# Seven products instead of eight for the up projection, on operands shared with q and k, and the down and out products moved behind it

## The chip, the cores and the metric

The kernel runs on one core of a Trainium2 chip. A core has a matrix engine (TensorE, PE in the profile), three engines for elementwise work (VectorE or DVE, ScalarE or ACT, GpSimd or POOL), a queue that issues most transfers (SyncE, SP), and 16 DMA engines between DRAM and the on-chip memory. Matrix products land in PSUM, which holds eight tiles of 128x512 numbers of 32 bits here. The metric is the device time of one execution in microseconds. All arithmetic is on 32-bit numbers.

## The reference

The input x has 2048 positions of 512 numbers. The kernel computes `x + s * silu(g)`, where s is a sliding attention over the normalised x and g a dense layer with squared ReLU over the same normalised x:

```python
xn = layernorm(x)                                   # 2048 x 512
q, k, v = split(xn @ wqkv)                          # 32 heads of 16
# every position looks back at 8 positions, 2 apart
logits = sum_d q[s] * k[s - 2*w] / 4                # w = 0..7; -1e9 before the start
o = sum_w softmax(logits)[w] * v[s - 2*w]
s = o @ wo                                          # 512 x 512
h = xn @ w1 + b1                                    # w1 is 512 x 1792, "up"
g = relu(h)**2 @ w2 + b2                            # w2 is 1792 x 512, "down"
out = x + s * silu(g)
```

## The kernel before, in words

**Numbers in two parts.** Each matrix operand is split into a high part of fewer bits (written by ACT) and the low part that is left (a subtraction on DVE or POOL). A product is then three matmuls, `PASSES`: high x high, high x low, low x high. A product over 512 input numbers is four slices of 128 of them times three passes, 12 matmuls of 128x512.

**Phase 1** goes over 16 tiles of 128 positions, in pairs. Each tile is normalised, transposed into `pxT` in PSUM, split into `xt` or `xT`, and multiplied with the weights of q, k and v. For the pairs in `SEVEN` (tiles 4 to 15) `pair_of_seven` (L800) computes the q and k of both tiles as a 2x2 block product with seven block products in place of eight, on sums of quarters of the two tiles (`copy_quarter`, `sums`, `high_sums`, `low_sums`) and sums of weights (`T1` to `T4`). For the pairs in `VSEVEN` (6 to 13) v is made in the same way, on halves of its columns. Results go through `stg` to DRAM (`sq`, `sk`, `sv`). The split operands of tiles 4 to 15 also go to DRAM (`sx`).

**Phase 2** goes over four chunks c of 512 positions, and over the 14 tiles f of 128 up features. `up(c, f)` (L604) is 12 matmuls of w1's tile with the chunk's operands `xT[c]`, loaded back from `sx`; then three passes on ACT make relu and the square, and POOL (in the first chunk DVE, for f = 2 to 11: `lowh`) the low part of h. `down` (L906) multiplies h of one f with w2, four position tiles by three passes. The four sums of a chunk stay in PSUM over all f. Up and down alternate on PE. `out_product` (L942) multiplies the attention's result with wo, tile by tile, between them; `finish` multiplies with the gate and adds x.

**Attention** needs no products: it is made by DVE alone, in `attention()` (L264), in eight units of 256 positions. A unit is four multiplies and four reductions for the logits (`qk`), the softmax (`soft_a`, `soft_b`, partly on POOL and ACT), and four multiplies and four reductions for the result (`av`). `load_u` fetches the unit's q, k and v from DRAM, and `store` writes the result to `so`, from where `load_o` (L917) fetches it for the out product; `trans_o` transposes it on DVE and `lowo` makes its low part there.

**The order of the work** is fixed when the program is built. Each engine runs its instructions in the order in which they were issued. A planner keeps two clocks, one for PE and one for DVE, with a price for each instruction. `pump(margin)` (L389) puts attention instructions into DVE's order as long as the DVE clock stays under PE's clock plus the margin: `LATE` (3.0 us) in phase 1, `ROOM0` (0.5 us) in the first chunk of phase 2, `ROOM` (3.5 us) in the others. `not_before(t)` moves the DVE clock forward where an instruction must wait for PE. `load_o(u, force)` with force places attention, whatever the clocks say, until unit u is stored:

```python
while done_units[0] <= u:
    flush(None)
    pump(clock["V"] - clock["PE"] + 4000)
```

`plan` holds what is done beside each step of a pair in phase 1 (`beside`). `queue` issues a transfer on SP in program order; a transfer that has to wait holds up those behind it.

Of the kernel before, what the change touches and what calls it, by code (L numbers as in the profile page):

```python
# [41 lines left out]
HOME = {0: 10, 1: K0, 2: T1, 3: T2, 4: T3, 5: Q0, 6: Q1, 7: K1, 8: T4, 9: V0, 10: V1}  # L42

SEVEN = range(4, 16, 2)
VSEVEN = range(6, 14, 2)
# [14 lines left out]
def body(ctx: ExitStack, tc: tile.TileContext, x, wqkv, wo, w1, b1, w2, b2, out):  # L60
# [48 lines left out]
    xTa = ctx.enter_context(tc.tile_pool(name="xTa", bufs=1))  # L109
    keep = ctx.enter_context(tc.tile_pool(name="keep", bufs=1))  # L110
    wts = ctx.enter_context(tc.tile_pool(name="wts", bufs=1))
    hpool = ctx.enter_context(tc.tile_pool(name="ph", bufs=1))
# [11 lines left out]
    def piece(name):  # L124
        return keep.tile([P, 512], F32, name=name, tag="z", bufs=4)
# [11 lines left out]
    p1ctx = ExitStack()  # L137
    px, pstg, pxT = (p1ctx.enter_context(tc.tile_pool(name=n, bufs=1)) for n in ("px", "pstg", "pxT"))
    xins = {}

# [15 lines left out]
    def load_x(t):  # L156
        xins[t] = px.tile([P, D], F32, name=f"x{t}", tag="x", bufs=4)
        queue(xins[t], tile_rows(x, t))
# [5 lines left out]
    wq = [buffer(f"wq{i}", i) for i in range(10)]  # L164
# [46 lines left out]
    b2t = const.tile([P, D], F32, name="b2t")  # L211
# [5 lines left out]
    sx = {c: dram.tile([P, KT, TPC, 2, P], F32, name=f"sx{c}") for c in range(1, NCH)}  # L217
# [185 lines left out]
    w12 = {}  # L403

    def load_w(f):
        r1, r2 = (piece(f"{n}{f}") for n in ("w1r", "w2r"))
        queue(r1.rearrange("p (k c) -> p k c", c=P), w1[:, f * P:(f + 1) * P].rearrange("(k p) c -> p k c", p=P))
        queue(r2, w2[f * P:(f + 1) * P, :])
        raws[f] = r1, r2

    def next_w():

        f = len(w12)
        if f < NF:
            w12[f] = buffer(f"w{f}", HOME[f]) if f in HOME else p2.tile([P, 2, 2, 512], FR, name=f"w{f}")
            for i, r in enumerate(raws.pop(f)):
                split(w12[f][:, 0, i], w12[f][:, 1, i], r, G)
            if f + 2 < NF:
                load_w(f + 2)
# [3 lines left out]
    mv, means, rs, shifts, xn, xb, pTs, xt, xT, seen, Sf, Sp, xts = ({} for _ in range(13))  # L423
# [11 lines left out]
    def spread(t):  # L435

        means[t], rs[t], shifts[t] = (small(n, t) for n in ("mean", "rs", "shift"))
        waste = hpool.tile([P, 512], F32, name=f"waste{t}", tag="hf")
# [11 lines left out]
    def norm(t):  # L450

        src = xins.pop(t)
        if t < TURN:
            xn[t] = dst = px.tile([P, 2, D], F32, name=f"xn{t}", tag="xb", bufs=2)[:, 0]
        else:
            if t % 2 == 0:
                xn[t] = px.tile([P, 4, 2, P], F32, name=f"xn{t}", tag="xn", bufs=2)
# [11 lines left out]
    def place(t):  # L469
        if t < TPC:  # L470
            parts = xT[0][:, :, t]
        else:
            parts = xts[t] = pxT.tile([P, KT, 2, P], FR, name=f"xt{t}", tag="xt", bufs=4)
        xt[t] = parts.rearrange("p k a n -> p a k n")

    def shuffle(t):

        src = xn.pop(t)
        xb[t] = px.tile([P, 4, 2, P], F32, name=f"xb{t}", tag="xb", bufs=2)
        for a in range(4):  # L480
            queue(xb[t][32 * a:32 * a + 32].rearrange("p b e c -> p b (e c)"), src[:, a].rearrange("p e c -> p (e c)"))
        if t > TURN:
            for i in range(t + 4, min(t + 6, NT)):
                load_x(i)

# [15 lines left out]
    def highx(t):  # L501
        A.activation(xt[t][:, 0], pTs[t].rearrange("p (k n) -> p k n", k=KT), AF.Copy)

    def lowx(t):
        not_before(seen[t])
        V.tensor_sub(xt[t][:, 1], pTs[t].rearrange("p (k n) -> p k n", k=KT), xt[t][:, 0].bitcast(F32))
# [8 lines left out]
    def copy_quarter(a):  # L515

        _, pb = quarters(a)
        Sf[a] = hpool.tile([P, 4, 2 * P], F32, name=f"Sf{a}", tag="h", bufs=4)
        A.activation(Sf[a][:, 3], pb[:, 0], AF.Copy)
        seen[a, "copy"] = clock["V"] + 1600  # L520

    def sums(a, half):

        f, (pa, pb) = Sf[a], quarters(a)
# [4 lines left out]
        else:  # L529
            V.tensor_sub(f[:, 2], pa[:, 0], f[:, 3])  # L530
            V.tensor_sub(f[:, 3], pa[:, 1], f[:, 1])
        seen[a, half] = clock["V"] + 900

    def sum_parts(a, half):
        n = 2 * half
        flat = Sf[a][:, n:n + 2].rearrange("p j m -> p (j m)")
        if (a, half) not in Sp:
            Sp[a, half] = hpool.tile([P, 2, 2, 2, P], FR, name=f"S{a}_{half}", tag="h", bufs=4)
        return (*(Sp[a, half][:, i].rearrange("p j k n -> p (j k n)") for i in range(2)), flat)
# [8 lines left out]
    def part_x(t, h):  # L548
        return lambda p, i: xt[t][:, p, 2 * h + i]

    def part_s(a, j):
        return lambda p, i: Sp[a, j // 2][:, p, j % 2, i]
# [13 lines left out]
    def new_stg(t, s):  # L566
        stgs[s] = pstg.tile([P, GR, 2, CH], F32, name=f"stg{t}_{s}", tag="stg", bufs=4)

    def qkv(t, s, between=None, late=False, new=True):
# [5 lines left out]
        for n, (kt, a, b) in enumerate(order):  # L575
            PE.matmul(ps, xt[t][:, a, kt], wq[2 * s + kt // 2][:, b, kt % 2, :], start=n == 0, stop=n == 11,
# [20 lines left out]
    def load_xT(c):  # L597
        xT[c] = xTa.tile([P, KT, TPC, 2, P], FR, name=f"xU{c}", tag="xT")
        for kt in range(KT):
            queue(xT[c][:, kt].bitcast(F32), sx[c][:, kt])  # L600

    hs = {}

    def up(c, f):  # L604
        ph = psH(f"ph{c}_{f}")
        n = 0
        for kt in range(KT):
            for a, b in PASSES:
                PE.matmul(ph.rearrange("p (j n) -> p j n", n=P), w12[f][:, a, 0, kt * P:(kt + 1) * P],
                          xT[c][:, kt, :, b, :], start=n == 0, stop=n == 11)  # L610
                n += 1
        if f == NF - 1 and c + 1 < NCH:
            load_xT(c + 1)
        h = hpool.tile([P, 2, 512], FR, name=f"h{c}_{f}", tag="h", bufs=4)
        A.activation(ph, ph, AF.Relu, bias=b1t[:, f:f + 1])
        A.activation(h[:, 0], ph, AF.Square)

        pool = c or f < 2 or f > 11
        full = hpool.tile([P, 512], F32, name=f"hf{c}_{f}", tag="hf") if pool else ph
        A.activation(full, ph, AF.Square)  # L620
        if pool:
            G.tensor_sub(h[:, 1], full, h[:, 0].bitcast(F32))
        hs[f] = h, None if pool else ph, clock["PE"] + 2000

    def lowh(f):
        h, ph, t = hs[f]
        if ph is not None:
            not_before(t)
            V.tensor_sub(h[:, 1], ph, h[:, 0].bitcast(F32))

# [12 lines left out]
    xT[0] = xTa.tile([P, KT, TPC, 2, P], FR, name="xT0", tag="xT")  # L643
# [8 lines left out]
    x0 = hpool.tile([P, D], F32, name="xT0f", tag="h", bufs=4)  # L652
# [6 lines left out]
    high(xt[0][:, 0], None, x0.rearrange("p (k n) -> p k n", k=KT))  # L659
    ps = psA("pq0_1")  # L660
    for kt in range(KT):
        if kt == KT - 1:
            trans(1)
        PE.matmul(ps, x0[:, kt * P:(kt + 1) * P], raws[1, kt], start=kt == 0, stop=kt == KT - 1)
    lowx(1)
    low(xt[0][:, 0], xt[0][:, 1], x0.rearrange("p (k n) -> p k n", k=KT), V)
# [12 lines left out]
    trans(2)  # L679
    lows(2, 0)  # L680
# [3 lines left out]
    trans(3)  # L684
    lows(2, 2)
# [23 lines left out]

    vl, vr = slice(0, 256), slice(256, 512)  # L710
    v_sums, v_parts = {}, {}

    def sum_v(n):
        dst, a, b = (((0, vl), (0, vr), (0, vl)), ((2, vr), (2, vr), (0, vl)), ((0, vr), (2, vr), (0, vr)),
# [385 lines left out]
```

## Time and profile before

| what | value |
|---|---|
| median of two runs | 484.75 us (484.53 and 484.98) |
| span of the profiled execution | 482.6 us; its own time is not listed apart from the two runs' |
| PE busy | 477.1 us, 2193 matmuls |
| DVE busy | 428.1 us, 356 instructions |
| ACT busy | 240.0 us |
| POOL busy | 221.8 us |
| moved by DMA | 81.47 MB |

The span goes from the first to the last instruction of the profiled execution. The profile page gives the busy time of each engine, a strip of 40 equal slices per engine (each digit the busy share in tenths), the costliest groups of instructions, and the chain of waits that ended last. In a group, `pb<-w,h` means that tile pb was written from w and h; then come the shape, the count, the busy time, the mean time of one and the idle time just ahead. All instructions that pass through the kernel's recording helper have the line number L91, so groups are told apart by the names of their tiles. A timeline row is start, duration, engine, line, operation, tiles, shape and count, and in brackets the engine's idle time before it with what ended it.

### The profile page before, as it was taken

How to read it: one execution, taken by the hardware profiler on the slowest of the kernel's cores; microseconds unless marked ns; L12 is line 12 of the kernel's file. 1: busy time of each engine (PE TensorE's matmuls, PEld its weight loads, DVE VectorE, ACT ScalarE, POOL GpSimd, SP SyncE). 2: the span in 40 equal slices, each digit the busy share in tenths (PEclk: the TensorE clock that was granted, in tenths of full speed). 3: DMA queues.
4: the chain of work that ended last, by engine and by line, in shares of the span. 5: the costliest groups of instructions: out<-in, count | busy, mean ns of one | idle time of the engine just before them, and what ended most of it. 6: DMA issues, size and time to landing. Idle time of an engine off the chain costs nothing.

```text
span 482.6 us, 6131 instructions
## 1 busy us (share of the span) xinstructions
PE 477.1 (99%) x2193; PEld 397.0 (82%) x2193; DVE 428.1 (89%) x356; ACT 240.0 (50%) x441; POOL 221.8 (46%) x174
## 2 busy tenths in 40 slices
PE   8999999999999999999999999999999999999996
PEld 6888888888888888888888888888888888888885
DVE  5968999899599999899999999999999999999133
ACT  5548798855566545463413345342235343423240
POOL 1459852116995654337445532653334257243210
PEclk9999999999999999999999999999999999999999
DMA  8999999998769765834624843560764446040331
GB/s 277 248 233 286 271 242 290 300 298 259 209 196 251 191 180 153 254 95 127 160 63 132 187 160 107 113 178 5 184 150 117 159 109 170 0 129 4 88 104 70
DMA packets 70890, 81.47 MB, mean 169 GB/s; under 512 B 6092, under 2 KB 55500, under 8 KB 70860
## 3 DMA queue, kind: packets, MB, share of 16 engines
q1 hardware_dynamic: 69564, 73.61, 55.3%
q10 hardware_dynamic: 1296, 7.47, 6.6%
q8 instruction: 17, 0.28, 0.2%
q14 instruction: 13, 0.11, 0.1%
HBM read 50.60 MB, written 27.32 MB: 161 GB/s over the span
## 4 chain that ended last, share of the span: by engine, by line
PE 98%; DMA 1%; DVE 0%; POOL 0%; issue 0%; POOLq 0%
PE pb L91 32%; PE ph L91 32%; PE pm L91 12%; PE pq L91 9%; PE pw L91 9%; PE pv L91 4%; DMA x<-in_A_x 1%; PE pxT L91 0%; DVE z L91 0%; DVE st L91 0%; POOL rs L91 0%; DVE xn L91 0%; DVE mv L91 0%; DVE rs L91 0%; PE warm L91 0%
## 5 line engine op out<-in xcount | busy, mean ns | idle before, releaser
L91 PE MATMUL pb<-w,h 128*128 128x512 f32 x672 | 160.1, 389 | 0.0
L91 PEld LDWEIGHTS pb<-w,h 128*128 128x128 f32 x672 | 126.1, 188 | 26.2
L91 POOL TENSOR_TENSOR h<-hf,h 128x512 fp32r<-128x512 f32 x46 | 72.2, 1570 | 133.7 <-ACT hf L91 133.6
L91 PE MATMUL ph<-xU,w 128*128 128x512 f32 x504 | 120.2, 389 | 0.0
L91 ACT ACTIVATE ph<-ph,b1t 128x512 f32<-128x512 f32 x56 | 37.1, 662 | 161.3 <-PE ph L91 161.3
L91 PEld LDWEIGHTS ph<-xU,w 128*128 128x128 f32 x504 | 94.6, 188 | 19.7
L91 DVE TENSOR_TENSOR pr<-k,q 128x2048 f32<-128x2048 f32 x32 | 79.4, 2480 | 0.9 <-DMA q<-sq 0.2
L91 DVE TENSOR_TENSOR pv<-v,L 128x2048 f32<-128x2048 f32 x32 | 78.4, 2450 | 1.3 <-POOL L L91 0.7
L91 DVE TENSOR_REDUCE v<-pv 128x256 f32<-128x2048 f32 x32 | 73.1, 2283 | 0.9
L91 DVE TENSOR_REDUCE L<-pr 128x128 f32<-128x2048 f32 x32 | 72.8, 2275 | 0.5
L91 PE MATMUL pw<-wot,oT 128*128 128x512 f32 (+1 forms) x204 | 45.9, 376 | 0.0
L91 PEld LDWEIGHTS pw<-wot,oT 128*128 128x128 f32 x204 | 36.8, 188 | 7.1
L91 PE MATMUL ph<-xT,w 128*128 128x512 f32 x168 | 40.0, 389 | 0.0
L91 POOL TENSOR_TENSOR w<-w1r,w 128x512 fp32r<-128x512 f32 x14 | 24.1, 1718 | 30.9 <-ACT w L91 29.3
L91 PEld LDWEIGHTS ph<-xT,w 128*128 128x128 f32 x168 | 31.5, 188 | 6.5
L91 PE MATMUL pm<-wq,S 128*128 128x512 f32 x144 | 36.5, 391 | 0.0
L91 ACT ACTIVATE h<-ph 128x512 fp32r<-128x512 f32 x56 | 33.7, 602 | 1.8
L91 PE MATMUL pq<-wq,xT 128*128 128x512 f32 x132 | 30.8, 392 | 0.0
L91 PEld LDWEIGHTS pm<-wq,S 128*128 128x128 f32 x144 | 26.3, 188 | 4.9
L91 PEld LDWEIGHTS pq<-wq,xT 128*128 128x128 f32 x132 | 24.5, 188 | 5.8 <-ACT xT L91 0.7
L91 ACT ACTIVATE hf<-ph 128x512 f32<-128x512 f32 x46 | 27.3, 594 | 1.3 <-POOL h L91 1.3
L91 PE MATMUL pm<-wq,xt 128*128 128x512 f32 x108 | 27.6, 392 | 0.0
(96 smaller groups left out, 534.5 us busy)
## 6 DMA issues: line engine op xcount, KB each, us to landing
sx<-xt SPq DMA_DIRECT2D x12, 512.0 KB, 7.0
xU<-sx SPq DMA_DIRECT2D x12, 512.0 KB, 6.3
k<-sk SPq DMA_DIRECT2D x5, 960.0 KB, 7.1
v<-sv SPq DMA_DIRECT2D x5, 960.0 KB, 7.1
x<-in_A_x SPq DMA_DIRECT2D x16, 256.0 KB, 8.0
sk<-stg SPq DMA_DIRECT2D x8, 512.0 KB, 4.2
sq<-stg SPq DMA_DIRECT2D x8, 512.0 KB, 7.7
sv<-stg SPq DMA_DIRECT2D x8, 512.0 KB, 5.0
```

What stands on the lines that cost most here:

```text
L91: return tc.keep_in_program_order(f(*a, **k))
```

## The change

The up projection is made by seven block products. A block pairs two tiles of w1 (pair g of 7) with the even and odd tiles of a group s of 1024 positions; the seven position operands are exactly those that q and k use in phase 1. They now live in four arrays `XA`, `XB`, `SA`, `SB`, with four slots each, one for each pair of tiles. Group 0 (tiles 0 to 7) is written to DRAM by `store_x` in phase 1; group 1 stays on the chip. The first four tiles get their sums too (`keep_full`, `early_sums`, `early_parts`). v is made by plain products in all pairs.

After phase 1 comes an up stage. Group 1 comes first, then `reload` brings group 0's operands back during the last call of group 1. Each call of `ups` takes two or three pairs g through the seven products; the pre-activations u go to DRAM in `su` (`give`). The sums of w1's tiles are made on the way (`plain_w1`, `sum_w1` on DVE from the third pair on, `sums_w1`). After that come the four chunks with only down and out products; u is loaded back (`load_ut`), squared by ACT, and its low part made by POOL (`make_h`), some tiles ahead. wo is split on POOL. The core of the diff:

```diff
-VSEVEN = range(6, 14, 2)
+JOINT = (((0, 1), (2, 3), (4, 5, 6)), ((0, 1, 2), (3, 4), (5, 6)))
...
-        return keep.tile([P, 512], F32, name=name, tag="z", bufs=4)
+        return keep.tile([P, 512], F32, name=name, tag="z", bufs=12)
...
+    XA = tpool.tile([P, 4, 2, 2, 256], FR, name="XA")
+    XB = tpool.tile([P, 4, 1, 2, 256], FR, name="XB")
+    SA = tpool.tile([P, 4, 2, 2, 256], FR, name="SA")
+    SB = tpool.tile([P, 4, 2, 2, 256], FR, name="SB")
+    operands = ((XA, 0), (XA, 1), (XB, 0), (SA, 0), (SA, 1), (SB, 1), (SB, 0))
...
+    sx = [dram.tile([P, 4, n, 2, 256], F32, name=f"sx{i}") for i, n in enumerate((2, 1, 2, 2))]
+    su = [dram.tile([NF, P, 2, 512], F32, name=f"su{s}") for s in range(2)]
...
+    def plain_w1(g):
+        r0, r1 = w1raws[g]
+        pool, tag, n = home(g, 1)
+        b = pool.tile([P, 2, 3, 256], FR, name=f"w1b{g}", tag=tag, bufs=n)
+        for cols, r in ((slice(0, 2), r0), (slice(2, 3), r1[:, 256:])):
+            r = r.rearrange("p (j m) -> p j m", m=256)
+            split(b[:, 0, cols], b[:, 1, cols], r, G)
+        w1s[g] = [b]
+
+    def sum_w1(g, eng):
+        r0, r1 = w1raws[g]
+        lo, hi = slice(0, 256), slice(256, 512)
+        eng.tensor_sub(r0[:, lo], r1[:, lo], r0[:, lo])
+        eng.tensor_sub(r1[:, lo], r1[:, hi], r1[:, lo])
+        eng.tensor_sub(r1[:, hi], r1[:, hi], r0[:, lo])
+        eng.tensor_sub(r0[:, hi], r0[:, hi], r1[:, hi])
...
+    def parts(t, src):
+
+        if t % 2 == 0:
+            return [(XA[:, slot(t), :, 0], XA[:, slot(t), :, 1], src.rearrange("p (h m) -> p h m", h=2))]
+        return [(odd[t][:, 0], odd[t][:, 1], src[:, :256]), (XB[:, slot(t), 0, 0], XB[:, slot(t), 0, 1], src[:, 256:])]
...
+    def keep_full(t, src):
+        f = fulls[:, t // 2]
+        for h, q in enumerate((3, 0) if t % 2 else (1, 2)):
+            A.activation(f[:, q], src[:, h * 256:(h + 1) * 256], AF.Copy)
...
+    for a, step, f, args in ((10, 2, load_w1, (0,)), (12, 0, load_w1, (1,)), (12, 4, plain_w1, (0,)),
+                             (12, 5, sum_w1, (0, G)), (14, 1, sums_w1, (0,)), (14, 2, load_w1, (2,)),
+                             (14, 2, plain_w1, (1,)), (14, 3, sum_w1, (1, G)), (14, 4, sums_w1, (1,))):
+        at(a, step, f, *args)
...
+    def multiply(ps, g, w, j, start):
+        t, n = operands[j]
+        w, k = (w1s[g][0], w) if w < 3 else (w1s[g][1], w - 3)
+        k0 = 0
+        for i in range(2):
+            cols = slice(i * P, (i + 1) * P)
+            for a, b in PASSES:
+                PE.matmul(ps.rearrange("p (j n) -> p j n", n=P), w[:, a, k, cols], t[:, :, n, b, cols],
+                          start=start and k0 == 0, stop=k0 == 5, skip_group_check=True)
+                k0 += 1
...
+        def take(g, i, e, ps):
+            us[g, i, e] = u = piece(f"u{s}_{2 * g + i}_{e}")
+            A.activation(u, ps, AF.Identity, bias=bias(g, i))
+
+        def give(g, i, e):
+            queue(su[s][2 * g + i][:, e], us.pop((g, i, e)))
...
+        def seventh(g):
+            multiply(X[g], g, 5, 5, False)
+            take(g, 1, 1, X[g])
+            G.tensor_add(us[g, 1, 1], us[g, 1, 1], five.pop(g))
+            give(g, 1, 1)
+
+        def third(g):
+            multiply(Z[g], g, 2, 6, False)
+            not_before(clock["PE"] + 300)
+            V.tensor_add(us[g, 1, 0], us[g, 1, 0], Z[g])
+            give(g, 1, 0)
...
+        order = ((first, second, sixth, fifth, seventh, third, fourth) if len(gs) > 2
+                 else (first, fifth, sixth, second, seventh, third, fourth))
+        for product_of in order:
+            for g in gs:
+                product_of(g)
+                for f in beside.pop(0) if beside else ():
+                    f()
+                pump(ROOM0)
+            if then:
+                then(product_of.__name__)
...
+    def prepare(step, g):
+        return ((step, plain_w1, g), (step + 1, sum_w1, g, V), (step + 4, sums_w1, g))
+
+    ups(1, JOINT[0][0], tasks(14, (0, load_w1, 3), *prepare(0, 2), (5, load_w1, 4), *prepare(7, 3)))
+    ups(1, JOINT[0][1], tasks(14, *prepare(0, 4), (1, load_w1, 5), *prepare(4, 5), (5, load_w1, 6), *prepare(9, 6)))
+    ups(1, JOINT[0][2], then=reload)
...
+    def make_h(c, f):
...
+        A.activation(u, u, AF.Relu)
+        A.activation(h[:, 0], u, AF.Square)
+        A.activation(u, u, AF.Square)
+        G.tensor_sub(h[:, 1], u, h[:, 0].bitcast(F32))
+        hs[c, f] = h
...
+        room = ROOM
+        for f in range(NF):
...
+            if f >= 7:
+                load_o(c * 2, f >= 9)
...
+            if f == 11:
                 for i in range(2):
                     trans_o(t0 + i, psT(f"pT{t0 + i}"))
+            if f == 12:
                 for i in range(2):
                     lowo(t0 + i)
+                load_o(c * 2 + 1, last)
+            ahead_h(c, f)
+            if f == 0 and c == 0:
+                pass
...
+            elif f < (NF - 3 if last else NF - 2):
+                for j in range(TPC):
+                    down(c, f, j)
             pump(room)
...
+            for i in range(2):
+                out_product(t0 + i, psH(f"pw{t0 + i}"))
+                pump(room)
             for i in range(2, TPC):
+                trans_o(t0 + i, psT(f"pT{t0 + i}"))
```

More of the change, by code (lines that the diff above doesn't have):

```diff
@@ L400, in pump @@
             not_before(limit)
[L403 to L419, printed above, removed]
+    w1s, w1raws = {}, {}
@@ L595, in store_qkv @@
         done[1][t // 2] = clock["PE"]
[L597 to L629, printed above, removed]
     def highs(s, kt):
@@ L663, in body @@
             trans(1)
+            keep_full(1, pTs[1])
         PE.matmul(ps, x0[:, kt * P:(kt + 1) * P], raws[1, kt], start=kt == 0, stop=kt == KT - 1)
     lowx(1)
-    low(xt[0][:, 0], xt[0][:, 1], x0.rearrange("p (k n) -> p k n", k=KT), V)
+    for part in parts(0, x0):
+        low(*part, V)
     evacuate(0, 1, ps)
```

427 lines of the change are left out of this document (223 added, 204 removed).

## The prediction

> **What bounds the kernel now.** I read the page first, then busy time by stage, the chain of waits in order of time, and the groups and timelines of single engines around the places that the change touches.
>
> ```profile
> span 482.6 us, 6131 instructions
> ...
> PE 477.1 (99%) x2193; PEld 397.0 (82%) x2193; DVE 428.1 (89%) x356; ACT 240.0 (50%) x441; POOL 221.8 (46%) x174
> ...
> PE   8999999999999999999999999999999999999996
> ...
> DVE  5968999899599999899999999999999999999133
> ```
>
> TensorE (PE) is never idle after the start, so fewer matmuls look like a gain one for one. But the second strip shows VectorE (DVE) nearly as full from slice 12 to slice 37. Busy time by stage, with the columns in the first line:
>
> ```profile
> core 0: us, PE busy (x) PEld busy (x) DVE busy (x) ACT busy (x) POOL busy (x), PEclk, DMA share, GB/s
> 45.00:130.00 85.00, 85.00 (x453) 73.35 (x453) 77.92 (x89) 63.27 (x139) 45.00 (x45) 1.00 0.98 274
> 130.45:265.00 134.55, 134.55 (x596) 111.40 (x595) 128.79 (x81) 66.73 (x117) 74.37 (x45) 1.00 0.60 163
> 265.00:446.30 181.30, 181.30 (x802) 150.12 (x801) 178.47 (x106) 73.27 (x123) 75.47 (x46) 1.00 0.45 119
> ```
>
> From 45 to 446.3 us DVE has 401.3 us and is busy 385.2; the largest single hole is one wait of 5.7 us, shown below. So DVE finishes the attention as soon as it can, and only what follows is slack. How much, the last unit of attention and the end show:
>
> ```profile
> 423.94 0.56 SPq L343 DMA_DIRECT2D so<-v  x1
> 443.93 2.29 DVE L91 TENSOR_REDUCE v<-pv 128x256 f32<-128x2048 f32 x1
> 446.24 0.55 SPq L343 DMA_DIRECT2D so<-v  x1
> 450.08 3.64 SPq L927 DMA_DIRECT2D oq<-so  x8
> 455.98 0.73 DVE L91 STREAM_TRANSPOSE pT<-oq 128x512 f32<-128x512 f32 x1 [8.57 <-ACT hf L91]
> 473.01 5.75 PE L91 MATMUL pw<-wot,oT 128*128 128x512 f32 x36
> ...
> oq<-so SPq DMA_DIRECT2D x64, 64.0 KB, 2.0
> ...
> L91 DVE TENSOR_TENSOR oT<-pT,oT 128x512 fp32r<-128x512 f32 x13 | 8.4, 680 | 1.5 <-ACT oT L91 1.5
> ```
>
> Attention ends at T = 446.2. Its result goes to DRAM and comes back: the loads are issued until 453.7 and land 2.0 later, at 455.7, T + 9.5. Two transposes (1.46) and the first low part (0.68) make T + 11.6; the last 36 products take 5.75; from their end (478.76) to the end of the span are 3.84. If only this chain were left, the end would be T + 21.2 = 467.4. PE has 15.2 us of work more than that now, and this is all that can be won before DVE bounds the kernel.
>
> **PE's side.**
>
> ```profile
> 86.10 2.75 PE pm L91 x12
> 100.78 2.75 PE pm L91 x12
> 282.77 5.44 PE pb L91 x24
> ```
>
> A matmul of 512 columns costs 5.44/24 = 0.2267 us. Up has 4 chunks x 14 tiles x 12 = 672 matmuls; seven products of six matmuls for 7 pairs of tiles and 2 groups are 588: 84 x 0.2267 = -19.0. A pair of position tiles with q, k and v by seven repeats after 14.68 us; q and k are 42 x 0.2267 = 9.52 of it, v 5.16. Plain v is 24 x 0.2267 = 5.44, four times +0.28 = +1.1. PE alone would end the span at 482.6 - 17.9 = 464.7.
>
> **DVE's side, which I think decides.** Groups between 45 and 446.3 us (busy, mean ns, idle before):
>
> ```profile
> L91 DVE TENSOR_TENSOR pr<-k,q 128x2048 f32<-128x2048 f32 x32 | 79.4, 2480 | 0.9 <-DMA q<-sq 0.2
> L91 DVE TENSOR_TENSOR pv<-v,L 128x2048 f32<-128x2048 f32 x32 | 78.4, 2450 | 1.3 <-POOL L L91 0.7
> L91 DVE TENSOR_REDUCE L<-pr 128x128 f32<-128x2048 f32 x32 | 72.8, 2275 | 0.5
> L91 DVE TENSOR_TENSOR xt<-pxT,xt 128x512 fp32r<-128x512 f32 x10 | 6.8, 683 | 0.0
> L91 DVE TENSOR_TENSOR h<-ph,h 128x512 fp32r<-128x512 f32 x10 | 6.8, 681 | 0.0
> L91 DVE TENSOR_TENSOR Sf<-Sf,pxT 128x256 f32<-128x256 f32 x10 | 4.1, 414 | 0.2
> L91 DVE TENSOR_TENSOR wot<-rwo,wot 128x512 fp32r<-128x512 f32 x4 | 4.2, 1079 | 0.0
> L91 DVE TENSOR_TENSOR stg<-stg,pm 128x512 f32<-128x512 f32 x6 | 4.1, 685 | 7.0 <-PE pm L91 6.9
> L91 DVE TENSOR_TENSOR stg<-stg,pv 128x256 f32<-128x256 f32 x4 | 1.7, 417 | 0.4 <-PE pv L91 0.4
> ```
>
> Work: gone are ten low parts of h (6.8), four of wo (4.3), four adds for v (1.7): -12.8. New are 14 adds in `third` (x 0.685 = 9.6), `sum_w1` on DVE for five pairs, 20 subtractions of 256 columns (x 0.414 = 8.3), and six odd tiles whose low part is now two halves (2 x 0.414 - 0.683 = 0.15 each, 0.9): +18.8. Net +6.0.
>
> Waits: DVE runs in the order that the planner wrote. In the up stage, attention is placed only until PE's planned time + ROOM0 (0.5 us) and in lumps of 2.3 (the reductions) to 2.5. The add in `third` reads PE's newest product, one product (6 x 0.2267 = 1.36) after the last placing. So DVE arrives 1.36 - 0.5 = 0.86 to 0.86 + 2.3 us early, 2.0 in the middle; attention queued behind the add waits with it. The add takes 0.6, the next pair's product ends 1.36 later, and no lump fits between: 0.76 for each further pair. Six calls x 2.0 + 8 further pairs x 0.76 = +18.1. The bounds are 0, if DVE always comes late, and 6 x 3.16 + 8 x 0.76 = 25. This stage has no row before, but the same kind of add has one:
>
> ```profile
> 119.43 2.29 DVE L91 TENSOR_TENSOR pr<-k,q 128x2048 f32<-128x2048 f32 x1
> 124.07 3.46 DVE L91 TENSOR_TENSOR pr<-k,q 128x2048 f32<-128x2048 f32 x1
> 133.26 0.69 DVE L91 TENSOR_TENSOR stg<-stg,pm 128x512 f32<-128x512 f32 x1 [5.73 <-PE pm L91]
> ...
> 125.34 3.35 POOL L91 TENSOR_TENSOR w<-w2r,w 128x512 fp32r<-128x512 f32 x1
> 129.91 1.30 POOL L91 TENSOR_TENSOR w<-w2r,w 128x512 fp32r<-128x512 f32 x1
> ```
>
> There DVE stood 5.73 us for PE, because up products lay inside the last pair; the change takes those out, so -5.7. I take the middle, 18.1, because at this wait DVE was on plan and not late.
>
> Contention: the same rows show a multiply of 3.46 beside a POOL subtraction of 3.35, against 2.29 and 1.30 apart. Over 64 multiplies the means exceed 2.285 by (0.195 + 0.165) x 32 = 11.5 us, at 195 us of POOL work (45.0 + 74.4 + 75.5): 0.059 per us. New for POOL are 21 more 256-column pieces of w1, eight for two `sum_w1`, 14 adds in `seventh`, ten h and four wo; gone are the v sums:
>
> ```profile
> L91 POOL TENSOR_TENSOR h<-hf,h 128x512 fp32r<-128x512 f32 x46 | 72.2, 1570 | 133.7 <-ACT hf L91 133.6
> L91 POOL TENSOR_TENSOR stg<-stg 128x256 f32<-128x256 f32 x4 | 3.4, 854 | 0.0
> L91 POOL TENSOR_TENSOR vsum<-wqraw,vsum 128x512 fp32r<-128x512 f32 x4 | 7.1, 1805 | 0.0
> ```
>
> 29 x 0.854 + 28 x 1.57 - 10.5 = +58 us, so +3.4. Bounds: 0, and 58 x 0.9 (1.17 lost per 1.30) x 0.39 (the multiplies' share of 401 us) = 20.
>
> The Trainium skill, "SBUF — State Buffer", section "Who interferes with whom", calls this an exclusive lock between the two engines in which the loser blocks fully. The pair of long rows agrees; by that rule the sum would lie toward the upper bound only if POOL mostly came first, and the mean of all multiplies says that it mostly does not.
>
> So far +6.0 + 18.1 - 5.7 + 3.4 = +21.8: unit 6 is stored at 423.9 + 21.8 = 445.7. In the last chunk the code forces `load_o(6)` at f = 9. PE's own work from there is 84 matmuls (19.0), the last 5.75 and 3.84, so this is at 464.7 - 28.6 = 436.1; with ROOM, attention placed up to 439.6 is not forced. Unit 6 is later, so the loop places attention to its store and little more, and the transposes at f = 11 follow at once: DVE stands for the round trip of 9.5 us, less one lump of up to 4 us that the loop places beyond. I take 6.0 (bounds 0 and 9.5). T = 446.2 + 21.8 + 6.0 = 474.0, the end 495.2. The two timed runs have a median of 484.75, 2.15 above this span: **497 us**.
>
> At nothing I cost: 8 copies `keep_full` (0.4 us each, under a DVE that starts attention at 45), and six ACT passes per pair and group, 84 x 0.6 = 50 us, covered by an ACT that is half idle; if that cover fails, PE stands and DVE behind it. `store_x`, `give`, `reload` and `load_ut` put about 32 MB more through SP's queue; attention's q, k, v loads stand behind each `give` that waits for ACT, POOL or DVE. That is a rival below.
>
> In the forecast PE stands over 10 us before its last products. The Trainium skill, "TensorE: Matmul & The Clock Gate", section "What's actually happening", says that after about 3.4 us idle the clock falls to half for about as long; an estimate from that page is +1.7 us, the sum 499 instead. Every window above has a granted clock of 1.00, and no run here shows it.
>
> **Rivals.** *Late adds absorb each other* (0.23): if POOL makes DVE late, half of the 18.1 is no loss of its own. T = 446.2 + 6.0 + 9.0 - 5.7 + 3.4 = 458.9, unit 6 at 436.6 isn't forced, end 480.1: 482. For it speaks the pair of long rows, against it that the lost time comes back as contention.
>
> *PE bounds after all* (0.20, the other side): the adds in `third` cost no wait, because DVE is always behind its plan there. Then T = 446.2 + 6.0 - 5.7 = 446.5, end 467.7: 470, and no less than PE's 464.7 + 2.15 = 467. It decides when DVE's net lateness is under 5.5 us. For it: PE is at 99% and the arithmetic saved is sure. Against: DVE is at 96% from 45 on, and program order fixes its waits.
>
> *The up stage starves* (0.12).
>
> ```profile
> sx<-xt SPq DMA_DIRECT2D x12, 512.0 KB, 7.0
> GB/s 277 248 233 286 271 242 290 300 298 259 209 196 251 191 180 153 254 95 127 160 63 132 187 160 107 113 178 5 184 150 117 159 109 170 0 129 4 88 104 70
> ```
>
> In the third call 7.3 MB of operands come back, 3.1 MB of pre-activations leave and some 2.2 MB of attention move in 21 x 1.36 = 28.6 us: 440 GB/s, where no slice shows over 300. At 300 it takes 42 us, up to 14 us late: 497 + 14 = 511. Against: each operand is asked for six steps, 24.5 us, before its next use.
>
> **Numbers.** The forecast has 0.45; it spans 490 to 505, and its size is worth 2% only above 494.4. A measurement here tells 2%: below 475.1 or above 494.4. Faster: 0.20. Within 2%: 0.23 + 0.08 = 0.31. Slower: 0.37 + 0.12 = 0.49. Both signs hold much, so the range goes from PE's bound, 467, to 514, which leaves out a part of the starved case and little else.
>
> **What would show it.** Up must have 588 matmuls and PE busy fall to about 459, with idle PE near the end. DVE's adds into u must show waits for PE, some 18 us in all; attention's last reduction must lie near 474; the transposes for tiles 12 and 13 must stand for the load of unit 6. I am wrong if the last reduction stays near 447, or if PE stands inside the up stage for ACT, POOL or a load.

## The result, and the profile after

The changed kernel takes 572.92 us (571.14 and 574.70) against 484.75: 1.182 times the time, with a 95% interval of 1.173 to 1.191. The forecast was 497 with a range of 467 to 514. Timed later in three rounds it took a median of 576.88 (574.25 to 580.64), 1.191 times (1.186 to 1.196). Its executions lie 6.4 us apart where those of the kernel before lie 0.6 apart, so of a version timed once a few us are no difference.

The page of the changed kernel:

```profile
span 572.9 us, 6280 instructions
...
PE 490.7 (86%) x2037; PEld 392.3 (68%) x2037; DVE 445.6 (78%) x380; ACT 300.6 (52%) x537; POOL 290.3 (51%) x224
...
PE   8996997999898879999984978999998999932905
...
DVE  5956855889477787969869759779996998994934
...
PEclk9997998999998979999997988999998999975957
```

No engine is full any more. PE has 156 matmuls fewer, as the sum had it, and yet 13.6 us more of busy time, for the most part because the clock that was 1.00 everywhere now is not. PE is busy for some 44 us at half clock, which loses about 22 us by estimate. Busy time in stretches of the changed kernel, with the columns in the first line: from the old start of attention to the new one, attention as a whole, its stages (from the old start through phase 1, up, down), and last a stretch inside the up stage.

```profile
core 0: us, PE busy (x) PEld busy (x) DVE busy (x) ACT busy (x) POOL busy (x), PEclk, DMA share, GB/s
45.08:53.13 8.05, 4.13 (x10) 3.27 (x11) 3.67 (x5) 6.39 (x15) 7.81 (x8) 0.64 0.72 155
53.13:546.60 493.47, 435.68 (x1810) 348.70 (x1808) 401.23 (x297) 264.95 (x465) 259.31 (x180) 0.94 0.69 200
45.08:149.10 104.02, 95.11 (x390) 75.51 (x391) 75.53 (x94) 61.15 (x131) 38.38 (x47) 0.95 0.83 230
149.10:310.40 161.30, 141.62 (x590) 113.58 (x588) 128.26 (x86) 79.75 (x136) 86.41 (x62) 0.95 0.77 240
310.40:546.60 236.20, 203.09 (x840) 162.88 (x840) 201.11 (x123) 130.44 (x213) 142.33 (x80) 0.92 0.58 159
205.89:261.50 55.61, 55.61 (x234) 45.82 (x235) 46.42 (x28) 22.62 (x35) 13.15 (x10) 0.95 0.92 302
```

The kernel before, from the start of attention to its end:

```profile
45.08:446.20 401.12, 401.12 (x1848) 335.13 (x1847) 385.00 (x275) 203.66 (x375) 195.14 (x135) 1.00 0.62 167
```

Attention ends at T = 546.6 in place of 446.2, 100.4 us later. Three numbers make this up. It starts 8.05 later; DVE has 401.2 - 385.0 = 16.2 more work; and it stands idle for 493.5 - 401.2 = 92.2 in place of 401.1 - 385.0 = 16.1, 76.1 more. The idle time is spread almost evenly over the three stages: 28.5, 33.0 and 35.1 us in the third to fifth row.

What DVE waited for during attention, in the changed kernel (total us, times, longest):

```profile
DVE w1r L98 <- POOL w1b L98: 15.9, 5, 6.7
DVE u L98 <- PE uZ L98: 15.1, 10, 3.7
DVE oT L98 <- ACT oT L98: 10.7, 3, 6.2
DVE stg L98 <- PE pm L98: 10.6, 5, 3.6
DVE XA L98 <- ACT XA L98: 9.9, 4, 4.6
DVE pT L98 <- DMA oq<-so: 9.7, 2, 7.9
DVE pv L98 <- DMA v<-sv: 9.2, 1, 9.2
```

Five of the seven are work that DVE does for PE (sums of weights, pre-activations, low parts, k), 62.2 us: at each of them it arrives before ACT, POOL or PE has delivered, and the attention queued behind stands with it. Before, only `stg` was over a few us.

The others are late for more than one reason. The longest wait, 6.72 us for `w1b`, ends at 159.15; through it POOL stood still for only 0.74 us and worked off what lay before it in its order. And POOL is slowed by the attention in its turn:

```profile
176.44 2.29 DVE L98 TENSOR_TENSOR pv<-v,L 128x2048 f32<-128x2048 f32 x1
...
176.46 3.39 POOL L98 TENSOR_TENSOR w1s<-w1r,w1s 128x512 fp32r<-128x512 f32 x1
```

The next such subtraction, at 179.82 with DVE idle, took 1.27; two more of this size, beside multiplies at 187.97 and 204.91, took 3.35 and 3.20. That the multiply is the cause is read from these times. Behind the 3.39 stand PE's wait of 2.37 us at 179.91 and DVE's of 3.63 at 182.36. The prediction priced this contention for DVE alone.

For `uZ` and `stg` DVE waits for PE, and PE itself is late. PE's timeline in phase 1 and the up stage, the longest rows with a wait in front (in brackets):

```profile
48.99 2.93 PE L98 MATMUL pm<-wq,SA 128*128 128x512 f32 x6 [4.56 <-ACT SA L98]
...
93.67 1.73 PE L98 MATMUL pq<-wq,odd 128*128 128x512 f32 x6 [3.42 <-ACT stg L98]
...
155.34 0.73 PE L98 MATMUL uZ<-SA,w1s 128*128 128x512 f32 x2 [1.99 <-ACT w1s L98]
...
179.91 1.65 PE L98 MATMUL uZ<-SA,w1s 128*128 128x512 f32 x4 [2.37 <-POOL w1s L98]
...
205.89 6.84 PE L98 MATMUL uY<-XA,w1b 128*128 128x512 f32 x18 [2.89 <-ACT uY L98]
...
310.40 9.92 PE L98 MATMUL pb<-w,h 128*128 128x512 f32 x36 [7.36 <-ACT pb L98]
```

By the prediction's own prices PE would have left phase 1 at 130.45 + 1.1 = 131.6 (the kernel before left it at 135.73 with 24 up products, 5.4 us, inside, so at 130.3 by itself) and begun the down products 588 x 0.2267 = 133.3 later, at 264.9. It began them at 310.4: 45.5 late, 17.5 of it in phase 1 and 28.0 in the up stage. In phase 1, 104.02 - 95.11 = 8.9 of it is idle time from 45.08 on, 6.7 is matmuls that took longer (390 x 0.2267 = 88.4 took 95.11), and by the other 1.9 PE was late already at 45.08; in the up stage 161.30 - 141.62 = 19.7 is idle and 141.62 - 133.3 = 8.3 longer matmuls. No single row is large but the last.

The end, from both engines' timelines of the changed kernel:

```profile
525.40 1.32 DVE L98 STREAM_TRANSPOSE pT<-oq 128x512 f32<-128x512 f32 x2 [7.92 <-DMA oq<-so]
...
544.26 2.29 DVE L98 TENSOR_REDUCE v<-pv 128x256 f32<-128x2048 f32 x1
555.97 1.32 DVE L98 STREAM_TRANSPOSE pT<-oq 128x512 f32<-128x512 f32 x2 [9.42 <-DMA oq<-so]
...
560.60 8.45 PE L98 MATMUL pw<-wot,oT 128*128 128x512 f32 x36 [17.46 <-DVE z L98]
```

The chain from the last reduction on is the one that was forecast, transposes after 9.4 us included, but it is 26.3 us long and not 21.2: the first of the last 36 products starts at T + 14.0 in place of T + 11.6, and after 17.5 us of idleness the 36 take 8.45 in place of 5.75. The row names what PE waited for: an add of DVE (`z`), which stood behind the transposes and the low parts and waited 1.21 us for ACT.

### The profile page after: what moved, and what is told of

Its sections match the earlier page's. It is cut to its first block, busy times and chain, and to the rows that moved or that the text cites. A ratio compares the mean times of both kernels' runs of the same rounds, so it can differ in the third digit from the quotient of the medians.

```text
span 572.9 us, 6280 instructions
## 1 busy us (share of the span) xinstructions
PE 490.7 (86%) x2037; PEld 392.3 (68%) x2037; DVE 445.6 (78%) x380; ACT 300.6 (52%) x537; POOL 290.3 (51%) x224
## 5 line engine op out<-in xcount | busy, mean ns | idle before, releaser
L98 POOL TENSOR_TENSOR h<-ut,h 128x512 fp32r<-128x512 f32 x56 | 98.8, 1773 | 52.4 <-ACT ut L98 48.6
L98 ACT ACTIVATE ut<-ut 128x512 f32<-128x512 f32 x112 | 67.9, 627 | 52.4 <-DMA ut<-su 50.6
L98 DVE TENSOR_TENSOR pv<-v,L 128x2048 f32<-128x2048 f32 x32 | 80.0, 2499 | 9.9 <-DMA v<-sv 9.2
L98 DVE TENSOR_TENSOR pr<-k,q 128x2048 f32<-128x2048 f32 x32 | 82.3, 2572 | 0.7
L98 ACT ACTIVATE u<-uX,b1t 128x512 f32<-128x512 f32 x42 | 28.6, 685 | 33.2 <-PE uX L98 24.4
L98 ACT ACTIVATE h<-ut 128x512 fp32r<-128x512 f32 x56 | 35.4, 632 | 10.6 <-PE pb L98 7.9
L98 POOL TENSOR_TENSOR u<-u,five 128x512 f32<-128x512 f32 x14 | 18.7, 1348 | 39.4 <-ACT u L98 39.4
L98 PE MATMUL pq<-wq,XA 128*128 128x512 f32 x132 | 33.4, 403 | 0.4 <-DVE wq L98 0.3
L98 POOL TENSOR_TENSOR w<-w2r,w 128x512 fp32r<-128x512 f32 x14 | 24.2, 1753 | 18.4 <-DMA w2r<-in_B_w 12.8
L98 PEld LDWEIGHTS pq<-wq,XA 128*128 128x128 f32 x132 | 25.6, 195 | 6.6 <-DVE wq L98 0.7
L98 POOL TENSOR_TENSOR w1s<-w1r,w1s 128x512 fp32r<-128x512 f32 x14 | 23.0, 1664 | 10.9 <-ACT w1s L98 10.9
L98 PE MATMUL uZ<-SA,w1s 128*128 128x512 f32 x84 | 22.2, 412 | 5.0 <-POOL w1s L98 3.0
```

Of the source, the lines that this page charges most:

```text
L98: return tc.keep_in_program_order(f(*a, **k))
```

## The experiments

All were timed once beside the kernel before (484.4 to 486.1), but for three, which were timed in three rounds. "Theory" is the reading above: DVE's order, written against PE's planned clock, sets the end, and each wait in it is paid.

### More attention placed ahead of each add in the up stage

```diff
-                pump(ROOM0)
+                pump(ROOM)
```

The margin says how far DVE's planned clock may run ahead of PE's while attention is placed. With the larger one attention comes earlier in DVE's order, and the adds of `third` later: in the traces 61 of the 128 multiplies and reductions of attention stand ahead of the last of these adds, in place of 54. Expectations below call this "only where it is 3.5 us behind"; the order in the traces is the other way round.

> In the up stage attention is placed up to 3.5 us ahead of TensorE in place of 0.5. Theory A: VectorE's waits for the product in the third step (15.1 us) fall under 5 and the total falls by 8 to 12, to about 562. Rival: VectorE then comes late to that add, TensorE stands for the buffer, and the waits for GpSimd's split of w1 (15.9 us) grow: 572 or more.

556.34, and in three rounds beside the changed kernel's 576.88:

> Attention placed in the up stage only where it is 3.5 us behind, timed again. Theory (15 us of waits of the add go, and the forced wait with them): a median of 550 to 557, 16 to 22 us under the changed kernel beside it. Rival (a lucky look): within 8 us of it.

553.99 (551.69 to 555.73), 1.143 times the kernel before (1.139 to 1.147). The waits of DVE in the first of these runs:

```profile
DVE w1r L98 <- POOL w1b L98: 16.2, 4, 6.8
DVE oT L98 <- ACT oT L98: 10.5, 4, 5.1
DVE XA L98 <- ACT XA L98: 9.7, 4, 4.7
DVE pv L98 <- DMA v<-sv: 8.4, 1, 8.4
DVE sm_None L98 <- ACT L L98: 8.0, 1, 8.0
```

The 15.1 us of waits for `uZ` have shrunk to under one, and the forced wait for unit 6 is gone with them, 24 us in all; 8.0 come back in a softmax that waits for ACT. T is 529.1, 17.5 earlier, although PE's first down product is later than before (324.2). So a constant in the placing is worth 23 us in the rounds, and T, not PE's start, decides.

### The add of `third` off DVE

```diff
-            G.tensor_add(us[g, 1, 1], us[g, 1, 1], five.pop(g))
+            G.tensor_add(us[g, 1, 1], us[g, 1, 1], five[g])
...
-            not_before(clock["PE"] + 300)
-            V.tensor_add(us[g, 1, 0], us[g, 1, 0], Z[g])
+            A.activation(five[g], Z[g], AF.Copy)
+            G.tensor_add(us[g, 1, 0], us[g, 1, 0], five.pop(g))
```

> The changed kernel, but the add of the seventh partial result in the up stage, which stood on VectorE and waited there for its product, is made by a copy on ScalarE and an add on GpSimd. Theory (VectorE's order sets the end, and what it waits for or does before the last reduction is paid in full): the 15.1 us of waits and 14 adds of 0.69 us, 9.7 us, leave VectorE, so 548 to 553. Rival (GpSimd and ScalarE are the pace of the up stage, and take longer with 14 instructions more each): the up stage ends later by what VectorE gains, 565 or more.

554.45, and timed in rounds:

> The add moved to ScalarE and GpSimd, timed again. Theory (its waits and 9.7 us of work leave VectorE): a median of 550 to 557, the same as the run beside it, as ScalarE and GpSimd give back what the work is worth. Rival: 545 or less, the work pays too; or within 8 us of the changed kernel, a lucky look.

555.27 (550.92 to 557.51), 1.145 times (1.140 to 1.150), the same as the run above. The same waits are removed by another way, which agrees with their price. Both gains are nets: in both versions DVE has a new wait of 8 to 9 us for ACT in a softmax. That 9.7 us of work left DVE too brings nothing on top.

Both together, meant with the next edit as well:

> All three together: the add on GpSimd, attention only where it is behind, attention ahead of the forced transposes. Theory: beside the 5 to 8 us of the forced wait, the 9.7 us of adds leave VectorE, whose waits in the up stage were already gone: 538 to 545. VectorE's work of about 390 us from 53 us on and the 26 us behind its last reduction leave no way below 485 by placing alone. Rival (the pace of ScalarE and GpSimd in the up stage decides): 550 or more.

562.64: the rival. It is slower than any execution of either alone. One wait, of 8.0 us in the run of 556.34, has grown:

```profile
DVE sm_None L98 <- ACT L L98: 17.9, 1, 17.9
```

It ends at 353.3, when ACT is squaring the pre-activations that come back from DRAM and stands for them (up to 4.56 us); the first down product is at 337.3. The edits don't add up.

### Work placed ahead of the forced transposes

```diff
+                pump(max(room, clock["V"] - clock["PE"] + 9500) if clock["V"] > clock["PE"] + room else room)
```

> The changed kernel with attention placed after each product of the up stage only where it is 3.5 us behind (as in the run that gave 556.3), and with 9.5 us of attention placed ahead of the forced transposes that wait for a round trip of their unit through memory. Theory: the forced wait of 7.9 us of the seventh unit is filled with work that VectorE has to do anyway, and the end comes 5 to 8 us earlier than 556.3: 548 to 552. Rival: the wait goes to the transposes' consumers on TensorE, or the next unit waits instead, 555 or more.

551.25, inside the theory's interval for a wrong reason. With the larger margin its condition never held: the order of all four engines came out the same as in the run of 556.34. The 5.1 us between the two are the scatter of one program, and say nothing about the round trip.

### The changed kernel again

> The changed kernel itself, timed again: 570 to 576, with a spread of its executions of about 5 us, as two equal orders showed; then single looks from 568 to 578 are no change. Rival: a spread under 1.5 us, and the looks at 578 were true losses.

576.88 with 6.4 us between its executions. The small differences below are judged by that.

### How much is attention's work

Here attention's multiplies and reductions are cut to an eighth or less (the attention in the output is not the reference's), first in the same order, then placed early by small planned prices, then the latter in the kernel before. One of the four cuts:

```diff
-            V.tensor_mul(pr, windows(k, i0, [[DIL * CH, W], [1, 4 * CH]]), qv)
+            V.tensor_mul(pr[:, 0], windows(k, i0, [[DIL * CH, W], [1, 4 * CH]])[:, 0], qv[:, 0])
```

> The attention's 64 multiplies and 64 reductions work on an eighth of their data or less (so its output is not the attention's); their order and the planner's prices stay. VectorE then has some 250 us less to do. Theory A (VectorE and its order bound the kernel): TensorE is left with 459 us of products and the stalls that it has by itself (staging 8, early sums 5, w1 6, first down products 10), 485 to 500 in all. Theory B (transfers or the other engines bound it): 540 or more.

524.82: neither. The last unit is still stored only at 496.2, and its waits and PE's start of the down products are:

```profile
DVE u L98 <- PE uZ L98: 61.0, 9, 19.5
DVE oT L98 <- ACT oT L98: 46.2, 6, 11.6
DVE z L98 <- PE pw L98: 37.1, 11, 6.2
DVE pv L98 <- DMA v<-sv: 26.5, 1, 26.5
```

```profile
298.77 22.41 PE L98 MATMUL pb<-w,h 128*128 128x512 f32 x86 [7.00 <-ACT pb L98]
```

DVE with almost nothing to do for attention waits for PE, since its order was written for PE's clock. And PE is still 298.8 - 264.9 = 33.9 late; DVE's load, with what POOL loses beside it, is behind only 11.6 of the 45.5. All of that is in the up stage: phase 1 ends at 149.7 here and at 149.1 with the whole attention, so its 17.5 are not from that load.

> The changed kernel with the attention's multiplies and reductions cut to an eighth or less (its output is not the attention's), and the planner given their true small prices, so that they lie early in VectorE's order. What is left is TensorE's own path with the other engines. Theory C (the stalls of phase 1 and of the up stage, 45 us of lateness at the first down product, come from GpSimd, ScalarE and the buffers and not from the attention): 495 to 510. Theory A alone (TensorE is late only behind VectorE): 466 to 475.

544.95, slower than with the late order. Its waits:

```profile
DVE z L98 <- PE pw L98: 63.6, 10, 10.5
DVE pv L98 <- DMA v<-sv: 57.8, 4, 18.4
```

Attention placed early waits for its v, up to 18.4 us at a time, and DVE's add for the up stage stands behind it; PE begins the down products at 329.4.

> The kernel before with the same cut of the attention (its output is not the attention's either). TensorE had no gap in it, so taking work from VectorE gives nothing: 482 to 485. If it falls under 478, VectorE did hold TensorE in a way that the trace does not show.

503.46, slower than the kernel before with all its work. There too DVE waited for v (22.7 us in 3 waits). Neither run measures a limit of PE, which is what they were made for; in both, work that waits early in an ordered queue went with a longer time than the same or more work done late.

### The preparation of the weights

```diff
-        return ((step, plain_w1, g), (step + 1, sum_w1, g, V), (step + 4, sums_w1, g))
+        return ((step, plain_w1, g), (step + 3, sum_w1, g, V), (step + 5, sums_w1, g))
...
-    ups(1, JOINT[0][1], tasks(14, *prepare(0, 4), (1, load_w1, 5), *prepare(4, 5), (5, load_w1, 6), *prepare(9, 6)))
+    ups(1, JOINT[0][1], tasks(14, *prepare(0, 4), (1, load_w1, 5), *prepare(4, 5), (5, load_w1, 6), *prepare(8, 6)))
```

> The sums of w1 on VectorE come three steps behind the plain split in place of one, their split five in place of four. Theory C: VectorE's waits for GpSimd's split (15.9 us) fall under 4, ScalarE's waits for the sums (13.8) fall, the first down product comes 5 to 10 earlier than 310.4 and the total falls by 10 to 16, to about 560. Rival: GpSimd itself is the pace of the up stage, and the waits only move to ScalarE and TensorE: 570 or more.

572.10, the rival: the wait of DVE for `w1b` halves (15.9 to 8.1), and the end does not move by more than the scatter.

With the sums left out altogether:

> The changed kernel without the four subtractions per group by which VectorE forms the sums of the up weights for groups 2 to 6 (20 instructions of 0.43 us and more, and the 15.9 us that VectorE waits for GpSimd ahead of them); the products run on the plain weights instead, so what comes out of the up stage isn't the reference's. Theory (VectorE's order is in the loop with TensorE, and its work and waits are paid at the end): 26 us less, 545 to 550. Rival (ring, stores, ScalarE and GpSimd hold the pace of the up stage, and another wait takes the place): 565 or more.

561.31, between the two. 13.9 us of work and 15.9 of waits are gone, but others grew:

```profile
DVE u L98 <- PE uZ L98: 27.0, 13, 8.6
DVE pv L98 <- DMA v<-sv: 21.0, 1, 21.0
```

With 11.9 us more for `uZ` and 11.8 more for v, most of the waits came back: DVE got earlier and PE only by 3.9 us (first down product at 306.5). On GpSimd in place of DVE, with the edits of the run of 551.25:

> The changed kernel with attention placed in the up stage only where it is 3.5 us behind, attention ahead of the forced transposes, and the weight sums of groups 2 to 6 on GpSimd instead of VectorE (20 instructions of 0.73 us there, as its own of groups 0 and 1 take). Theory: 9 to 12 us of VectorE's work and up to 16 us of its waits go, against 551.3: 535 to 543, still above the 484.6 of the kernel before. Rival (GpSimd, which does the low parts of the weights in the same order, gets later and TensorE with it): 548 or more.

552.93, the rival. The wait goes to ACT and from there to PE, whose longest stand in the up stage is now 8.03 us for a pre-activation (4.60 in the run of 551.25):

```profile
ACT w1s L98 <- POOL w1r L98: 39.4, 7, 9.6
```

### Small causes in phase 1 and at the first down product

```diff
-        stgs[s] = pstg.tile([P, GR, 2, CH], F32, name=f"stg{t}_{s}", tag="stg", bufs=3)
+        stgs[s] = pstg.tile([P, GR, 2, CH], F32, name=f"stg{t}_{s}", tag="stg", bufs=4)
```

> Theory A: the end follows VectorE's last attention reduction (546.6 us, then 26 us), so idle time taken from VectorE ahead of it comes off the total. With four staging buffers for q, k and v in place of three (and ten pieces in place of twelve, for the room), ScalarE's wait for the store of k (14.3 us) and of v (3.5 us) goes; phase 1 ends some 8 to 12 us earlier than 149.1, the total falls to 555 to 565. Theory B: the idle time moves to the next wait, because the transfers are the bound (113 MB): total 568 or more.

578.06. Phase 1 ends 3.4 us sooner (145.7), but the first down product is later (313.9). The ring of pieces had to shrink from 12 to 10 for the room, and the run does not tell the two effects apart. No gain, as theory B had it, but not shown to be for its reason, and no loss beyond the scatter.

```diff
-        at(a, step + 1, early_parts, p, G)
+        at(a, step + 3, early_parts, p, G)
```

> The split of the early sums is issued two steps later, so that ScalarE does not stand for GpSimd's sums ahead of the first seven-product pair. Theory A: ScalarE's 6.0 us wait and TensorE's 4.6 us stall go, the attention starts near 47 instead of 53, the total falls by 5 to 7, to about 567. Theory B: no change, 571 to 575.

581.03, neither, and at the upper edge of the scatter. The 4.56 us in front of `SA` are gone, and PE stands twice as long 12 us on, since the normalised tile needs the buffer that the sums still hold:

```profile
59.94 0.81 ACT L98 ACTIVATE turn<-x,shift,rs 128x512 f32<-128x512 f32 x1 [11.11 <-POOL SB L98]
...
61.28 2.93 PE L98 MATMUL pq<-wq,odd 128*128 128x512 f32 x6 [9.86 <-ACT stg L98]
```

```diff
-        at(a, step, early_sums, p, G)
-        at(a, step + 1, early_parts, p, G)
+        at(a, step, early_sums, p, V)
+        at(a, step + 1, early_parts, p, V)
```

> The early sums and their low parts are made by VectorE in place of GpSimd. Theory C: ScalarE's wait for GpSimd's sums (6.0 us) goes, and with it TensorE's 4.6 us stall and the half clock behind it; phase 1 ends 5 to 8 earlier than 149.1, the attention starts by 50 in place of 53, the total falls by 5 to 9, to about 565. Rival: VectorE, which now does 6 us more, only moves the same stall: 571 or more.

574.26, the rival: nothing beyond the scatter.

```diff
+    b2t = const.tile([P, D], F32, name="b2t")
...
-    b2t = p2.tile([P, D], F32, name="b2t")
```

> The changed kernel, but the bias of the down product is loaded in phase 1 to a place of its own (for room the ring of pieces goes from 12 to 11), so that nothing but ScalarE's order stands ahead of the first down product. Theory (VectorE's order sets the end, not TensorE's start): the 7.4 us wait of TensorE falls or moves, and the end by no more than 4 us, 568 to 575. Rival: TensorE's lateness there goes on to the end in full: 564 to 567.

578.47, above both and inside the scatter, with the same 7.37 us at the first down product (now at 312.9). The bias's load was not what it waited for: ACT comes to it behind twelve passes of `make_h` and two of the up stage, back to back from 303.7 to 312.3. The run does not tell what that wait is worth.

### Plain v alone, in the kernel before

```diff
-VSEVEN = range(6, 14, 2)
+VSEVEN = range(0)
```

> The kernel before with one part of the change alone: v of the four pairs of tiles that had seven products for it is made by plain products. What the prediction priced: 1.1 us more of TensorE, which does not set the end, so 484 to 488. Rival: plain v by itself makes phase 1 late (its staging and its stores stand differently), and is behind a part of the 17.5 us by which phase 1 of the changed kernel ended late; then 492 or more.

486.98 against 484.63: the price of plain v is small, and phase 1's delay is not from it alone.

## Why the prediction was wrong

It was right that the kernel would be slower and that DVE's last reduction would decide; it gave the time 76 us too little. By its own steps:

**PE alone would end at 464.7.** The count held (156 matmuls fewer). The step that failed is "at nothing I cost": ACT's and POOL's new passes "covered by an ACT that is half idle". ACT is busy 52% and POOL 51%, and still PE stood for them, 8.9 + 19.7 = 28.6 us in phase 1 and the up stage: the share of busy time does not say when a pass comes. Three of the rows above tell why. At the first down product (7.36) ACT had passes of `make_h` in front in its order; at 179.91 (2.37) POOL was slowed beside DVE's multiply; at 93.67 (3.42) ACT itself had stood 6.43 us for a store of k to free its buffer. PE was 45.5 late at the first down product, which alone puts its own end at 464.7 + 45.5 = 510.2. "PE stands inside the up stage for ACT, POOL or a load" was named as what would make the prediction wrong, and it did.

**DVE's work, +6.0 and +3.4 of contention.** It is +16.2. The multiplies' means (2572 and 2499 ns) exceed 2285 by 16.0 us in all against 11.5, so their contention is +4.5, right in size. `sum_w1` was mis-sized: 20 subtractions took 13.9 and not 8.3, because eight of them lie beside POOL, which the price from another tile's subtraction did not have (the last section). With these 5.6 us, contention costs DVE about 10 us, in the middle of the bounds 0 and 20.

```profile
L98 DVE TENSOR_TENSOR pr<-k,q 128x2048 f32<-128x2048 f32 x32 | 82.3, 2572 | 0.7
L98 DVE TENSOR_TENSOR pv<-v,L 128x2048 f32<-128x2048 f32 x32 | 80.0, 2499 | 9.9 <-DMA v<-sv 9.2
...
L98 DVE TENSOR_TENSOR w1r<-w1r,w1r 128x256 f32<-128x256 f32 x15 | 9.8, 656 | 16.5 <-POOL w1b L98 15.9
...
L98 DVE TENSOR_TENSOR w1r<-w1r 128x256 f32<-128x256 f32 x5 | 4.1, 816 | 0.2
```

**Waits of `third`, +18.1.** 15.1 in ten waits, and two edits that take them away, by different ways, win 21 to 23 us together with the forced wait that hangs on them. The mechanism was right, and its size nearly.

**The wait in the last pair, -5.7.** `stg` waited 6.9 before and 10.6 after. The wait of the last pair fell from 5.73 to 2.79, but there are now five waits in place of three, the longest (3.56) in an earlier pair; what makes DVE early there was not tested.

**Forced `load_o(6)`, +6.0.** 7.92 at the place that was named, and 1.81 at the unit before, 9.7 in all. Right.

**Not in the sum at all:** attention's start, 8.05 late, as the low part of the first sums waits behind POOL and ACT (DVE idle 3.9 there, PE 4.56); DVE's waits for `w1b` (15.9), for ACT's high parts `XA` (9.9) and `oT` (10.7, where 1.5 stood before), and for v (9.2; 0 before). With the 1.5 taken off, the five are 52.3 of the 72.6 us by which T was forecast too early (546.6 against 474.0). By kind the 72.6 are 8.05 of later start, 16.2 - 9.4 = 6.8 of work and 57.7 of idle time beyond the 18.4 that the three waits of the sum come to.

**The end, T + 21.2.** T + 26.3. 2.7 of the 5.1 is the slow clock, which the prediction gave 1.7 in a sentence beside the sum and left out of it.

**The rivals.** The starved up stage (511) did not happen where it was expected: from 205.89 to 261.50, the rest of the call that brings the operands back and the call behind it, PE has no idle time, at 302 GB/s. The one wait for v (9.2) comes after the up stage, at 335.95. PE bounding after all (470) did not happen, and late adds that absorb each other (482) only in part: the four adds of the first two calls, where DVE stood for `w1b` before, had no wait, and the other ten had the 15.1.

**What is not settled.** With DVE nearly freed of attention's work, PE is still 33.9 late at the first down product. Idle time and longer matmuls are told apart above; how much of it is the ring of pieces, how much the passes of ACT and POOL, and how much the transfers is not. Edits at single places that PE stood for gave nothing beyond the scatter or moved the wait, so it is shown only that no one of those places is the cause by itself. Of the 76.1 us of idle time that DVE has more, two edits by different ways win 21 to 23; the rest is read from waits and not shown by a run. The fastest of the versions timed in rounds lies at 554, 14% over the kernel before.

## What to carry to other kernels

When a stage is changed so that each product needs passes on other engines before the next can go, price the loop in order, product by product: a half-idle engine covers nothing if the pass stands behind another in its order, for a buffer, or beside an engine that slows it. Where one engine's order is written against another's planned clock, lateness of either can become a wait of the other; check the plan's clock against the trace at each stage's border first. Time such a kernel several times before believing a few us: the scatter grew from 0.6 to 6.4 us.

## What the runs showed of the hardware that was not expected

The clock of PE falls at short waits. After 4.56 us idle, six products took 2.93 us, where such a row of six otherwise reads 1.52; after 2.89, eighteen took 6.84 in place of 4.24; after 17.46, 36 took 8.45 in place of 5.75. After 3.42 the first six took 1.73 and the next twelve 4.43 in place of 2.88. The granted clock behind the 2.37 us at 179.91, in the columns of the windows above:

```profile
180.45:183.75 3.30, 3.30 (x9) 2.58 (x8) 1.36 (x2) 0.60 (x1) 2.56 (x3) 0.50 1.04 363
```

In this trace the clock was at half for a stretch with every idle time of PE of 1.87 us or more, and with none of 1.63 or less. The Trainium skill, "TensorE: Matmul & The Clock Gate", section "What's actually happening", says half clock after an idle window of some 3.4 us. The trace agrees at 4.56 and differs at 1.87 to 2.89. The length alone does not decide: in the run of 524.82 the same eighteen products took 4.39 behind 2.90 us. In phase 1 and the up stage longer matmuls make 6.7 + 8.3 = 15.0 us, a third of PE's delay; PE was busy some 20 us at half clock there, so by estimate about 10 of them are the clock.

Eight of the 20 subtractions of `sum_w1` run beside POOL, and pay for it. The timeline of both engines in the changed kernel:

```profile
157.84 1.96 POOL L98 TENSOR_TENSOR w1b<-w1r,w1b 128x512 fp32r<-128x512 f32 x2
...
159.15 0.94 DVE L98 TENSOR_TENSOR w1r<-w1r,w1r 128x256 f32<-128x256 f32 x1 [6.72 <-POOL w1b L98]
160.12 0.43 DVE L98 TENSOR_TENSOR w1r<-w1r 128x256 f32<-128x256 f32 x1
...
168.76 2.91 POOL L98 TENSOR_TENSOR u<-u,five 128x512 f32<-128x512 f32 x2
169.13 1.40 DVE L98 TENSOR_TENSOR w1r<-w1r 128x256 f32<-128x256 f32 x1
```

With POOL idle a subtraction of 256 columns takes 0.43 us (twelve of them); the first of each four starts while POOL is still at its last `w1b` and takes 0.94; three beside POOL's adds take 1.33 to 1.40. The mean of all twenty is 0.70. That POOL is the cause is read from these times and was not tested apart.
